# Arc tangent of the first unit ahead of its decay sums, one h chunk in a bank of attention, new due times

## The chip, the cores and the metric

The kernel runs on one core of one Trainium2 chip. The metric is the device time of one execution in microseconds (us). Five engines work side by side, each through its own list of instructions: TensorE (PE, matrix products), ScalarE (ACT, functions of one element from a table of functions that has to be loaded), VectorE (DVE), GpSimd (POOL, hardly used here) and SyncE (SP, which issues the transfers). An engine takes its instructions strictly in the order of its list; an instruction that waits holds back all behind it.

## The reference

There are two stages. The first is a gated linear attention over 4 batches, 8 heads, 768 steps and 48 dimensions: a complex state per head is turned and shrunk by a gate at every step, k times v is added to its real part, and q reads it.

```python
mag = np.sqrt(a_re * a_re + a_im * a_im)
scale = np.minimum(mag, 0.999) / (mag + 1e-06)
a_re_n, a_im_n = (a_re * scale, a_im * scale)
for t in range(S):
    new_re = ar * S_re - ai * S_im
    new_im = ar * S_im + ai * S_re
    S_re, S_im = (new_re + kv, new_im)      # kv = outer product of k_t and v_t
    y[:, :, t] = np.einsum('bhd,bhde->bhe', q[:, :, t], S_re)
```

Its result, 3072 tokens of 384, goes through two matrix products with a smooth ramp between: `h = x @ w_in` (384 to 2048), `g = h` where h >= 1, 0 where h <= -1 and `(h + 1)**2 / 4` between, and `out = g @ w_out`.

## The kernel before

**Units, blocks, gates.** The 3072 tokens are cut into 12 units of 256 steps of one batch; two units make a block of 512 tokens, and there are six blocks. `gates(u)` works out a unit's gate: the logarithm of its size (the decay) and its angle. Instead of stepping through time it forms running sums of both. For units 0 and 1 (`by_token`) PE does that with a triangular matrix of ones (`running`, L772, tile `tri`), for the others DVE does it with a scan (L798). From a sum of decays come exponentials (ACT, L826 for units 0 and 1), from a sum of angles sine and cosine, and DVE multiplies q and k by them (L840, L935). The gated heads `hd` are laid out anew by transfers on SP (L505).

**The function tables.** Ln and Exp live in one table set, arc tangent and sine in another. `table(name)` (L515) loads a set on ACT; L1418 loads the first. In `gates`, Ln, Exp, Square, Ln, Exp (all recorded by the helper `ac`, L715) work out the decay, with products on DVE between them (L729, L736, L745); the arc tangent needs the slope (imaginary over real part) that L729 makes. In this kernel `gates(0)` and `gates(1)` are generators that stop at `yield`; the last lines of the program step them in turn, with the table loads between, so that units 0 and 1 share each load.

**Attention.** `attend(u)` computes for each half of a unit the scores (L1089), masks them on DVE (L1101), transposes k (L1029), multiplies with v (L1141), reads the state (L1133) and updates it (L1058; the state is added up on DVE, L1068 and L1070). Its results lie in six banks of PSUM: `at0` to `at2` and `o0` to `o2`. `split` moves the values into the shape of tokens and cuts them into a rounded part xH (ACT, L1236) and a remainder xL (DVE, L1243).

**The two products.** `moe(blk)` works through 16 chunks f of 128 columns of h. `gemm1(f)` (L1269) is nine matrix products of 128x512 (three pieces, each xH by two parts of the weight and xL by one) into one of two banks, `h0` and `h1`, taken in turn; ACT makes s from h (L1295), DVE makes g from h and s (L1314, the last reader of the bank), ACT rounds it (gh, L1328), DVE takes the remainder (gl, L1332), and `gemm2` (L1346) adds gh and gl by w_out into `o0` to `o2`. In block 0 the first two chunks (HALVES = 2) are worked in halves, one per unit.

**Weights.** They arrive coded; `weights` decodes a piece in three steps on DVE (L535, L544, L553), rounds it on ACT (L559) and, for the first five pieces, forms the remainder on PE (L573 and L574, in bank `h0`), copied by ACT (L588); for later pieces DVE forms it (L564).

**What sets the order.** Nothing is issued as written. `Plan` records every operation with its cost, its engine and what it needs, works out backwards when each is due, and then lets each engine take, of what is ready, the operation due first. The table NUDGE adds a number of nanoseconds to the due time of the operation with that index. `emit` writes the order out and fills gaps of PE's plan with filler products (`warm`, L1409: a 128x128 product into bank `h1` that nobody reads) until the first chunk of h.

## Time and profile before

| what | us |
|---|---|
| median of three runs | 565.61 |
| the three runs | 565.61, 563.85, 566.46 |
| the profiled execution | 562.77 |
| its span, first to last instruction | 561.0 |
| PE busy in it | 549.5 |
| DVE busy | 438.1 |
| ACT busy | 396.1 |

The profile is of one execution. "Busy" counts the time in which an engine worked on something, filler products too. PE's matrix products are pipelined: one record starts before the one before it has ended, so durations of a row may add up to more than the time from one row's start to the next; the starts tell how long a group took. A 128x128 product of full precision leaves two records in the trace, so 41 filler products are 82 records. A bracket at the end of a row gives the idle time of the engine before it and the instruction that ended it.

### The profile page before, as it was taken

The page shows a single profiled execution, that of the slowest core. Times are in us where ns is not written, and L with a number is a line of the kernel's source. Part 1 is how long each engine was busy: PE and PEld are TensorE (multiplying, and loading weights), DVE is VectorE, ACT ScalarE, POOL GpSimd, SP SyncE. Part 2 cuts the span into 40 slices and gives each one's busy share as a digit, 9 for nine tenths or more (in the row PEclk, how much of TensorE's full clock was granted, in tenths as well). Part 3 has the DMA queues.
Part 4 walks back from the last instruction along what each step waited for, and adds up shares of the span by engine and source line. Part 5 has one row for each costly group of instructions (what it writes and reads, how often), then busy time and mean ns, then how long its engine had stood idle before and what let it go on. Part 6 is the DMA issues. An engine that isn't in the chain of part 4 may idle for free.

```text
span 561.0 us, 10737 instructions
## 1 busy us (share of the span) xinstructions
PE 549.5 (98%) x4256; PEld 461.1 (82%) x4256; DVE 438.1 (78%) x611; ACT 396.1 (71%) x638; POOL 4.1 (1%) x27
## 2 busy tenths in 40 slices
PE   8999799999999999999999999999999999999997
PEld 8978688788788888888888888888888888888885
DVE  5899999999978798788897758796888645445554
ACT  6987998989976667757757565557665752369973
POOL 2000000000000000000000000000000000000000
PEclk9999999999999999999999999999999999999999
DMA  8678384554711705405300552602635400087613
GB/s 339 251 231 270 115 288 163 177 220 161 227 58 49 224 4 154 158 21 147 129 1 4 160 169 76 200 2 66 209 115 161 171 1 1 27 317 276 232 63 110
DMA packets 23686, 80.56 MB, mean 144 GB/s; under 512 B 4560, under 2 KB 10320, under 8 KB 23632
## 3 DMA queue, kind: packets, MB, share of 16 engines
q1 hardware_dynamic: 23488, 79.71, 43.0%
q8 instruction: 34, 0.56, 0.4%
q14 instruction: 20, 0.16, 0.1%
q10 hardware_dynamic: 144, 0.13, 0.1%
HBM read 55.05 MB, written 4.72 MB: 107 GB/s over the span
## 4 chain that ended last, share of the span: by engine, by line
PE 84%; DVE 7%; DMA 4%; SPq 2%; ACT 1%; issue 1%; POOL 0%; DVEq 0%; POOLq 0%; ACTq 0%
PE o L1346 33%; PE h L1269 32%; PE at L1089 4%; PE idle L1409 3%; PE at L1133 3%; PE at L1141 3%; PE at L1058 2%; SPq L505 2%; DMA raw_o<-in_wl_dram 2%; PE at L1029 1%; PE o L772 1%; DMA out_dram<-ob 1%; DVE g L1314 1%; DMA kq<-in_kq_dram 1%; DVE x L935 1%
## 5 line engine op out<-in xcount | busy, mean ns | idle before, releaser
L1269 PE MATMUL h<-xH,wi 128*128 128x512 f32 (+1 forms) x588 | 181.3, 390 | 4.0 <-DVE g L1314 3.4
L1346 PE MATMUL o<-gh,wo 128*128 128x512 f32 x576 | 179.7, 393 | 0.0
L1269 PEld LDWEIGHTS h<-xH,wi 128*128 128x128 f32 x588 | 107.5, 188 | 27.3 <-DVE g L1314 4.2
L1346 PEld LDWEIGHTS o<-gh,wo 128*128 128x128 f32 x576 | 106.8, 188 | 22.5 <-DVE wo L564 0.5
L1269 PE MATMUL h<-xL,wi 128*128 128x512 f32 (+1 forms) x294 | 113.7, 387 | 0.0
L1346 PE MATMUL o<-gl,wo 128*128 128x512 f32 x288 | 112.3, 390 | 0.0
L1328 ACT CAST gh<-g 128x512 fp32r<-128x512 f32 x96 | 59.5, 620 | 56.5 <-DVE g L1322 27.4
L1314 DVE TENSOR_TENSOR g<-h,s 128x512 f32<-128x512 f32 x96 | 65.9, 686 | 40.2 <-ACT s L1295 38.3
L1295 ACT ACTIVATE s<-h,cst 128x512 f32<-128x512 f32 x96 | 65.6, 686 | 36.7 <-PE h L1269 28.2
L1332 DVE TENSOR_TENSOR gl<-g,gh 128x512 fp32r<-128x512 f32 x96 | 65.4, 684 | 26.9 <-PE o L1346 21.1
L1269 PEld LDWEIGHTS h<-xL,wi 128*128 128x128 f32 x294 | 55.2, 188 | 11.7 <-DVE xL L1243 0.4
L1346 PEld LDWEIGHTS o<-gl,wo 128*128 128x128 f32 x288 | 54.1, 188 | 11.3
L1322 DVE SCALAR_TENSOR_TENSOR g<-s,g 128x512 f32<-128x512 f32 x80 | 55.2, 690 | 2.1
L715 ACT ACTIVATE ai<-ai 128x768 f32<-128x768 f32 x48 | 40.2, 844 | 10.6 <-DVE ai L878 5.0
L1101 DVE COPY_PREDICATED am<-tri,at 128x512 f32<-128x512 uint32 x44 | 31.9, 740 | 7.7 <-PE at L1089 7.1
L798 DVE TENSOR_TENSOR_SCAN ai<-again,ai 128x768 f32<-128x768 uint8 x20 | 35.0, 1750 | 0.3
L1089 PEld LDWEIGHTS at<-hd 96*64 96x64 f32 x704 | 31.3, 137 | 3.9 <-issue 3.2
L1089 PE MATMUL at<-hd 96*64 96x128 f32 (+1 forms) x704 | 33.9, 249 | 0.0
L1141 PE MATMUL at<-am,V 128*64 128x128 f32 x352 | 32.9, 273 | 0.1
L1133 PE MATMUL at<-hd,st 96*64 96x128 f32 x304 | 30.5, 278 | 0.1
L515 ACT ACT_TABLE_LOAD x23 | 29.5, 1283 | 0.4
L715 ACT ACTIVATE x<-ai 128x768 f32<-128x768 f32 x27 | 22.1, 840 | 8.8 <-DVE ai L798 8.5
(127 smaller groups left out, 637.5 us busy)
## 6 DMA issues: line engine op xcount, KB each, us to landing
chk<-in_wl_dram SPq DMA_DIRECT2D x16, 768.0 KB, 5.4
kq<-in_kq_dram SPq DMA_DIRECT2D x12, 768.0 KB, 4.8
ai<-in_ari_dram SPq DMA_DIRECT2D x10, 768.0 KB, 6.0
V<-in_v_dram SPq DMA_DIRECT2D x12, 576.0 KB, 4.1
hd<-x SPq DMA_DIRECT2D x24, 288.0 KB, 3.3
hd<-kq SPq DMA_DIRECT2D x24, 288.0 KB, 4.2
raw_i<-in_wl_dram SPq DMA_DIRECT2D x8, 768.0 KB, 5.5
raw_o<-in_wl_dram SPq DMA_DIRECT2D x8, 768.0 KB, 6.0
```

Of the source, the lines that this page charges most:

```text
L715: lambda: A_.activation(out(), src(), f, **kw),
L798: lambda: V_.tensor_tensor_scan(dst().rearrange("p j t -> p (j t)"), again, src().rearrange("p j t -> p (j t)"), 0.0, op0=ALU.mult, op1=AL ...
L1089: PE_.matmul(SC.get()[o : o + HC, i + e, HC * k :], t[:, 0, ks], t[:, 1, qs], start=True, stop=True,)
L1133: PE_.matmul(o_, st.get().rearrange("p h e -> p (h e)")[:, lo : lo + 64], head(h)[:, 1, cs], start=True, stop=False,)
L1141: PE_.matmul(o_, V.get()[:, c, lo : lo + 64], ams[pr // 2].get()[:, 2 * (pr % 2) + e, :], start=st is None, stop=True,)
L1269: PE_.matmul(H.get()[:, lo:hi], weight["i", f // 2].get()[:, f % 2, part, sl], x.get()[:, j, lo:hi], start=j == 0 and n == 0, stop=j == NJ ...
L1295: lambda: A_.activation(SS.get(), H.get(), AF.Relu, bias=c_half, scale=-0.5 if spare else 0.5),
L1314: lambda: V_.tensor_tensor(G.get(), H.get(), SS.get(), op=ALU.max),
L1322: lambda: V_.scalar_tensor_tensor(G.get(), SS.get(), 1.0, G.get(), op0=ALU.min, op1=ALU.mult),
L1328: pl.op("ACT", act(T), lambda: A_.copy(GH.get(), G.get()), r=[G], w=[GH])
L1332: lambda: V_.tensor_tensor(GL.get(), G.get(), GH.get().bitcast(F32), op=ALU.subtract),
L1346: PE_.matmul(PO[m].get(), weight["o", f // 2].get()[:, f % 2, part, sl], g.get(), start=f == 0 and n == 0, stop=f == NF - 1 and n == 2,)
```

## The change

There are three edits. First, `gates(0)` stops twice more: its Square, and its arc tangent right behind, now come behind the slope's product (L729) with a load of the angle table ahead and a load of the logarithm table after them. So there are two more table loads, 24 become 26 with the first one. The remaining steps of `gates(0)` are recorded ahead of the last ones of `gates(1)`. Second, in block 0 chunk f=2 (SIDE) takes its bank from attention's three in turn (here `at0`) instead of from h's two; the chunks behind it take `h0` and `h1` in turn, so chunk 3 has `h0` and chunk 4 `h1`. Third, the table NUDGE has other numbers throughout, with which the planner puts all engines' work in another order.

```diff
@@ NUDGE
-    18: 15300, 20: -28200, 60: -152000, 61: 9200, 68: -300, 70: 500, 71: -17000, 96: -113000,
...
+    13: -203753000000, 17: -203724995000, 27: -896426000, 28: -202829000000, 29: -202829000000,
...
 HALVES = 2
+SIDE = (2,)
@@ gates
         ve(dve(N), lambda: V_.tensor_tensor(I(), I(), A(), op=ALU.mult), [a], [i])
+        if u == 0:
+            yield
         ac(A, I, AF.Square, [i], [a])
+        if u == 0:
+            ac(I, I, AF.Arctan, [a], [i], True)
+            yield
...
         if u > 1:
             table("trig_and_small")
+        if u > 1:
+            arctan()
         if u != 1:
-            arctan()
             yield
@@ gemm1
-            H = tl(turn_of("h", 2), [P, T], F32, f"h_{blk}_{f}", ps)
+            slot = turn_of(*("at", 3) if blk == 0 and f in SIDE else ("h", 2))
+            H = tl(slot, [P, T], F32, f"h_{blk}_{f}", ps)
@@ the end of the program
     first, second = gates(0), gates(1)
     next(first)
+    table("trig_and_small")
+    next(first)
+    table("natural_log_exp_and_others")
+    next(first)
     next(second)
     next(first)
     table("trig_and_small")
     next(first)
     next(second)
+    list(first)
     table("natural_log_exp_and_others")
     next(second)
     table("trig_and_small")
-    list(first)
     attend(0)
     list(second)
     attend(1)
```

In the rows of the two orders that follow, a tile's name has its number behind it, and the line numbers of the kernel after are smaller by 13 to 24, since its table is shorter.

PE at the start of the program, before. `idle` is the filler, `ai_0` and `ai_1` are the gates of units 0 and 1, `tri` the triangle of ones; `o0` and `o1` take the sums of decays, `o2` and `at2` those of angles:

```order
L1409 MATMUL idle_171<-tri_69,ident_64 128x128 x41
L772 MATMUL o0_112<-tri_69,ai_0_132 128x256
L772 MATMUL o0_112<-tri_69,ai_0_132 128x128
L772 MATMUL o0_112<-tri_69,ai_0_132 128x256
L772 MATMUL o0_112<-tri_69,ai_0_132 128x128
L772 MATMUL o1_113<-tri_69,ai_0_132 128x256
L772 MATMUL o1_113<-tri_69,ai_0_132 128x128
L1409 MATMUL idle_171<-tri_69,ident_64 128x128 x15
```

and after:

```order
L1392 MATMUL idle_167<-tri_69,ident_64 128x128 x41
L753 MATMUL o2_114<-tri_69,ai_0_132 128x256
L753 MATMUL o2_114<-tri_69,ai_0_132 128x128
L753 MATMUL o2_114<-tri_69,ai_0_132 128x256
L753 MATMUL o2_114<-tri_69,ai_0_132 128x128
L753 MATMUL at2_111<-tri_69,ai_0_132 128x256
L753 MATMUL at2_111<-tri_69,ai_0_132 128x128
L1392 MATMUL idle_167<-tri_69,ident_64 128x128 x18
L753 MATMUL o0_112<-tri_69,ai_0_132 128x256
```

The angle sums of unit 0 (o2, at2) have moved ahead of 18 fillers, and the decay sums (o0, o1), which stood right behind the first filler, come after them. The sums of unit 1, which were among the first, now come later, between products of weights' remainders.

ACT at the start, before (`x_0` and `x_1` are the decays of the two units, written by Ln):

```order
L715 ACTIVATE x_0_151<-ai_0_132,cst_86 128x3x256
L715 ACTIVATE ai_0_132<-x_0_151 128x768
L715 ACTIVATE ai_0_132<-ai_0_132 128x768
L715 ACTIVATE ai_0_132<-ai_0_132,cst_86 128x768
L715 ACTIVATE x_1_161<-ai_1_135,cst_86 128x3x256
L715 ACTIVATE ai_1_135<-x_1_161 128x768
L715 ACTIVATE x_0_151<-x_0_151,cst_86 128x3x256
L715 ACTIVATE ai_1_135<-ai_1_135 128x768
L715 ACTIVATE ai_1_135<-ai_1_135,cst_86 128x768
```

and after:

```order
L691 ACTIVATE x_0_151<-ai_0_132,cst_86 128x3x256
L691 ACTIVATE ai_0_132<-x_0_151 128x768
L491 ACT_TABLE_LOAD
L691 ACTIVATE ai_0_132<-ai_0_132 128x768 x2
L491 ACT_TABLE_LOAD
L691 ACTIVATE ai_0_132<-ai_0_132,cst_86 128x768
L691 ACTIVATE x_1_220<-ai_1_139,cst_86 128x3x256
L691 ACTIVATE ai_1_139<-x_1_220 128x768
L691 ACTIVATE x_0_151<-x_0_151,cst_86 128x3x256
```

Two table loads now stand around unit 0's Square and arc tangent (the row with x2). Unit 1's steps have moved behind them. Later in the list, between unit 0's exponentials and attention, ACT has three table loads, as before. Up to attention four weight pieces are cast instead of three, two of them ahead of unit 0's exponentials; the last copies of remainders before the first scores are those of weight i2, where before they were those of o0.

On SP, the first loads were those of the gates of units 0 and 1, then kq of unit 0, then weights i0 and i1; after, the gate of unit 0, weights i0 and i1, then the gate of unit 1, kq of unit 0 and weight i2.

PE at chunk 2 of block 0, before (the end of the second halves of chunks 0 and 1, then chunk 2 and the first products by w_out):

```order
L1269 MATMUL h_0_1_692<-xH_0_638,wi_0_289 128x256 x2
L1269 MATMUL h_0_1_692<-xL_0_682,wi_0_289 128x256
L1269 MATMUL h_0_2_778<-xH_0_638,wi_1_309 128x512 x2
L1269 MATMUL h_0_2_778<-xL_0_682,wi_1_309 128x512
L1269 MATMUL h_0_2_778<-xH_0_638,wi_1_309 128x512 x2
L1269 MATMUL h_0_2_778<-xL_0_682,wi_1_309 128x512
L1269 MATMUL h_0_2_778<-xH_0_638,wi_1_309 128x512 x2
L1269 MATMUL h_0_2_778<-xL_0_682,wi_1_309 128x512
L1346 MATMUL o0_112<-gh_0_0_784,wo_0_346 128x512 x2
```

and after:

```order
L1252 MATMUL h_0_1_737<-xH_0_683,wi_0_254 128x256 x2
L1252 MATMUL h_0_1_737<-xL_0_711,wi_0_254 128x256
L1252 MATMUL at0_109<-xH_0_683,wi_1_227 128x512 x2
L1252 MATMUL at0_109<-xL_0_711,wi_1_227 128x512
L1252 MATMUL at0_109<-xH_0_683,wi_1_227 128x512 x2
L1252 MATMUL at0_109<-xL_0_711,wi_1_227 128x512
L1252 MATMUL at0_109<-xH_0_683,wi_1_227 128x512 x2
L1252 MATMUL at0_109<-xL_0_711,wi_1_227 128x512
L1252 MATMUL h_0_3_813<-xH_0_683,wi_1_227 128x512 x2
L1252 MATMUL h_0_3_813<-xL_0_711,wi_1_227 128x512
L1252 MATMUL h_0_3_813<-xH_0_683,wi_1_227 128x512 x2
```

Chunk 2 has gone from a bank of h to `at0`, and chunk 3 in `h0` follows it at once, ahead of the products by w_out.

DVE from the end of attention of units 0 and 1 to g of chunk 0, before (L887 `state` stands just ahead of the first row):

```order
L1243 TENSOR_TENSOR xL_0_682<-xr_0_442,xH_0_638 128x3x256
L535 TENSOR_SCALAR y_i3_689<-raw_i3_482 128x768
L544 SCALAR_TENSOR_TENSOR raw_i3_482<-raw_i3_482,y_i3_689 128x768
L553 SCALAR_TENSOR_TENSOR raw_i3_482<-raw_i3_482 128x768
L1243 TENSOR_TENSOR xL_0_682<-xr_0_442,xH_0_638 128x256
L935 TENSOR_TENSOR x_2_380<-kq_2_475,ai_2_153 128x1536
L1243 TENSOR_TENSOR xL_0_682<-xr_0_442,xH_0_638 128x256 x2
L935 TENSOR_TENSOR kq_2_475<-kq_2_475,ai_2_153 128x1536
L564 TENSOR_TENSOR wi_3_755<-raw_i3_482,wi_3_755 128x2x384
L1070 TENSOR_TENSOR st_1_611<-st_1_611,o0_112 96x384
L1314 TENSOR_TENSOR g_0_0_771<-h_0_0_718,s_0_0_760 128x512
```

and after (`st` is the state's sum, `xL` the remainder of x, `kq` and `x` the turned q and k of unit 2, `raw` and `y` steps of decoding weights):

```order
L1052 TENSOR_TENSOR st_1_637<-st_1_637,o0_112 96x384
L869 TENSOR_SCALAR state_108<-ai_2_158 128x3
L1225 TENSOR_TENSOR xL_0_711<-xr_0_467,xH_0_683 128x3x256
L540 TENSOR_TENSOR wi_3_662<-raw_i3_375,wi_3_662 128x2x384
L520 SCALAR_TENSOR_TENSOR raw_o2_605<-raw_o2_605,y_o2_705 128x768
L917 TENSOR_TENSOR x_2_405<-kq_2_529,ai_2_158 128x1536
L1225 TENSOR_TENSOR xL_0_711<-xr_0_467,xH_0_683 128x256 x3
L917 TENSOR_TENSOR kq_2_529<-kq_2_529,ai_2_158 128x1536
L705 TENSOR_TENSOR ai_3_532<-ai_3_532 128x768
L529 SCALAR_TENSOR_TENSOR raw_o2_605<-raw_o2_605 128x768
L1297 TENSOR_TENSOR g_0_0_805<-h_0_0_722,s_0_0_777 128x512
```

The state's sum, which stood just ahead of g, now comes first; the decoding of weight i3 has been done earlier, and a product of unit 3 (L705) and steps of weight o2 stand ahead of g.

## Rows read from the trace of the kernel before

**Rows 1.** From the page: busy time of the engines (share of the span, instructions), and the granted clock of PE in 40 equal slices of the span, in tenths of full speed (9 is 90% or more).

```profile
PE 549.5 (98%) x4256; PEld 461.1 (82%) x4256; DVE 438.1 (78%) x611; ACT 396.1 (71%) x638; POOL 4.1 (1%) x27
...
PEclk9999999999999999999999999999999999999999
```

**Rows 2.** PE's timeline from the start to the first scores. Columns: start, time until the group's end, engine, line, operation, output from inputs, shape, count of records, idle time before.

```profile
1.82 11.74 PE L1409 MATMUL idle<-tri,ident 128*128 128x128 f32 x82 [1.82 <-POOL tri masks.py:66]
13.40 2.13 PE L772 MATMUL o<-tri,ai 128*128 128x256 f32 x12
15.36 3.51 PE L1409 MATMUL idle<-tri,ident 128*128 128x128 f32 x30
18.81 2.88 PE L772 MATMUL o<-tri,ai 128*128 128x256 f32 x16
...
37.04 1.56 PE L1089 MATMUL at<-hd 96*64 96x128 f32 x32
```

**Rows 3.** ACT's timeline up to attention, the same columns.

```profile
8.74 0.92 ACT L715 ACTIVATE x<-ai,cst 128x768 f32<-128x768 f32 x1
...
14.91 1.09 ACT L826 ACTIVATE x<-o 128x512 f32<-128x512 f32 x2 [1.53 <-PE o L772]
...
16.83 0.94 ACT L715 ACTIVATE x<-x,cst 128x768 f32<-128x768 f32 x1
17.78 1.28 ACT L515 ACT_TABLE_LOAD   x1
19.08 1.58 ACT L715 ACTIVATE ai<-ai 128x768 f32<-128x768 f32 x2
...
21.97 1.73 ACT L826 ACTIVATE x<-o 128x512 f32<-128x512 f32 x4
...
27.45 0.94 ACT L715 ACTIVATE ai<-ai,cst 128x768 f32<-128x768 f32 x1
...
35.46 0.48 ACT L588 CAST wo<-rest_o 128x384 fp32r<-128x384 f32 x1 [0.37 <-PE rest_o L574]
```

**Rows 4.** ACT's instructions grouped by line and shape over the whole span. Columns: group and count, busy us and mean ns of one, idle us before.

```profile
L715 ACT ACTIVATE ai<-ai 128x768 f32<-128x768 f32 x48 | 40.2, 844 | 10.6 <-DVE ai L878 5.0 <-DVE ai L729 3.3 <-DMA ai<-in_ari_dram 2.1
L515 ACT ACT_TABLE_LOAD x23 | 29.5, 1283 | 0.4
...
L559 ACT CAST wi<-raw_i 128x768 fp32r<-128x768 f32 x8 | 7.3, 906 | 0.1
...
L588 ACT CAST wi<-rest_i 128x384 fp32r<-128x384 f32 x6 | 2.8, 469 | 1.2 <-PE rest_i L574 1.2
```

**Rows 5.** PE's timeline from the end of attention of units 0 and 1 to the first product by w_out.

```profile
59.10 0.94 PE L573 MATMUL rest_o<-raw_o,ident 128*128 128x384 f32 x2
...
60.06 0.40 PE L1269 MATMUL h<-xH,wi 128*128 128x256 f32 x2
...
66.43 0.28 PE L1269 MATMUL h<-xL,wi 128*128 128x256 f32 x1
69.35 0.73 PE L1269 MATMUL h<-xH,wi 128*128 128x512 f32 x2 [2.64 <-DVE g L1314]
...
71.52 0.62 PE L1346 MATMUL o<-gh,wo 128*128 128x512 f32 x2
```

**Rows 6.** SP's issues of the moves of unit 0's heads and of the last moves of x before block 0.

```profile
31.24 3.43 SPq L505 DMA_DIRECT2D hd<-kq  x5
...
58.81 3.81 SPq L505 DMA_DIRECT2D xr<-xr  x6
```

**Rows 7.** PE's two later waits for DVE.

```profile
109.28 0.72 PE L1269 MATMUL h<-xH,wi 128*128 128x512 f32 x2 [0.54 <-DVE g L1314]
...
332.80 0.73 PE L1269 MATMUL h<-xH,wi 128*128 128x512 f32 x2 [0.21 <-DVE g L1314]
```

**Rows 8.** DVE's timeline: the first step on unit 0's angle sums, and the stretch from the end of attention to g of chunk 0 and a little behind.

```profile
22.36 0.68 DVE L854 TENSOR_SCALAR ai<-o 128x512 int32<-128x512 f32 x1
...
59.13 0.17 DVE L887 TENSOR_SCALAR state<-ai 128x3 f32<-128x3 f32 x1
59.44 0.96 DVE L1243 TENSOR_TENSOR xL<-xr,xH 128x768 fp32r<-128x768 f32 x1
...
63.11 1.75 DVE L935 TENSOR_TENSOR x<-kq,ai 128x1536 f32<-128x1536 f32 x1
64.77 0.75 DVE L1243 TENSOR_TENSOR xL<-xr,xH 128x256 fp32r<-128x256 f32 x2
...
67.11 0.95 DVE L564 TENSOR_TENSOR wi<-raw_i,wi 128x768 fp32r<-128x768 f32 x1
67.98 0.54 DVE L1070 TENSOR_TENSOR st<-st,o 96x384 f32<-96x384 f32 x1
68.60 0.69 DVE L1314 TENSOR_TENSOR g<-h,s 128x512 f32<-128x512 f32 x1
69.21 0.55 DVE L535 TENSOR_SCALAR y_o<-raw_o 128x768 uint32<-128x768 uint32 x1
69.67 0.95 DVE L729 TENSOR_TENSOR ai<-ai 128x768 f32<-128x768 f32 x1
```

**Rows 9.** Two stretches: its bounds, its length, busy us (and instructions) of PE, PE's weight loads, DVE, ACT and POOL, granted clock, share of the transfer engines, GB/s.

```profile
4.13:35.94 31.81, 30.60 (x204) 27.34 (x203) 25.33 (x35) 26.88 (x37) 0.77 (x4) 1.00 0.76 288
5.00:10.00 5.00, 5.00 (x39) 5.00 (x39) 1.92 (x2) 3.82 (x6) 0.00 (x0) 1.00 1.01 412
```

87 rows, old and new, of the table NUDGE are left out of this document.

## The prediction

> **What bounds the kernel now.** I read the page's busy shares first [rows 1]: TensorE (PE) is busy for 98% of the span at a granted clock that reads 9 (90% or more) in all 40 slices, so an edit pays only if it takes work or a wait from PE. The waits of PE come next: 2.64 us before chunk 2 of block 0 [rows 5], 0.54 and 0.21 us later [rows 7], all ended by DVE's product g. The rest of PE's loss is idle filler (L1409) in the opening and counts as busy, so it is seen only in PE's row of time: 82 filler records until 13.40 and 30 more from 15.36 [rows 2]. Behind the gap of 2.64 us PE has work in hand until the end but for those two small waits. The time is therefore set by when the gap's end is reached and by what PE has done by then; I work out that one point for both kernels.
>
> **The opening: decay sums later.** Before, unit 0's decay sums stand directly behind the first filler, at 13.40, and 30 filler records follow them. After, the angle sums stand there (possible because the arc tangent comes early), then 18 fillers (36 records), and only then the decay sums. Twelve records of sums cost 15.36 - 13.40 = 1.96; a filler record costs 3.45/30 = 0.115 (15.36 to 18.81). So the decay sums start at 13.40 + 1.96 + 36 x 0.115 = 19.5, which is 6.1 later. ScalarE's (ACT's) first exponential of a decay comes 14.91 - 13.40 = 1.51 behind the sums' start, so at 21.0, and they end as before 16.83 - 14.91 = 1.92 later, at 22.9 [rows 2, 3].
>
> **The two table loads.** One is 1.283 us, with the next activation right behind it (17.78 + 1.28, then 19.08) [rows 3, 4]. I cost the pair, 2.57, at nothing, because ACT waits there for PE's sums: everything that ACT has to do before the exponentials is ready earlier. The last piece hangs on DVE: angle sums end at 15.36, DVE's step on them takes 0.68, then a product of 0.95 [rows 8], then Square 0.84, Ln 0.94 and a cast 0.91 [rows 3, 4], which gives 19.7 against 21.0. Unit 1's inputs are now queued on SP behind two weight loads of 768 KB; at the 412 GB/s of that stretch [rows 9] these are 1.9 us each, and what needs them first (8.7 before) slips to 12.5 at the most, still ahead. If that cover of 1.3 us is gone, the loads cost up to 1.3 us of the 2.57.
> The Trainium skill, "ScalarE: Activation LUTs", section "What ACT_TABLE_LOAD costs", gives about 1283 ns for the load and about 1380 ns of drain at every switch of set. The rows above show the first figure and no drain. By the Trainium skill the two early loads would be 2.76 us more of ACT, so 22.4 against 21.0, and the end 1.4 later.
>
> **ACT up to attention.** Behind unit 0's exponentials ACT now has, until the copy of the first half of weight i2's remainder: two Ln or sine steps with a pointer (0.94), seven copies of remainders (0.47), three table loads (1.283), five activations of 0.844, two casts (0.906) and unit 1's exponentials (1.73) [rows 3, 4]: 1.88 + 3.29 + 3.85 + 4.22 + 1.81 + 1.73 = 16.8. It ends at 22.9 + 16.8 = 39.7. Before, the matching copy (wo) ended at 35.46 + 0.48 = 35.94, with ACT busy for 26.9 of the 31.8 us up to there [rows 3, 9]. From that copy to the first scores were 37.04 - 35.94 = 1.10; after, four fillers more (8 x 0.115 = 0.9): attention starts at 41.7, that is s = 4.7 later. The other bound on that start is the moves of unit 0's gated heads: their cosine ends at 22.9 + 8.0 = 30.9 against 28.4, so they land 2.5 later than before, at 39.6 if the last was as late as 37.04 [rows 3, 6]; it does not decide. So s lies between 0 (PE's later sums fully absorbed, the floor if everything else is as before) and 6.1 (all passed on); the sum of ACT's durations gives 4.7 and I take it.
>
> **From attention to the gap.** Attention of units 0 and 1 took 59.10 - 37.04 = 22.06 with two remainder products in it; it has two afterwards as well, so it ends at 63.8, and h0 begins after 1.15 of filler instead of 0.96 of remainder products [rows 5]. What PE then waits for is bank h0, freed by DVE's g0. Behind attention's end DVE has: state sum 0.54, state 0.17, xL 0.96, a weight sum 0.95, a decode step 0.95, the turn of x 1.75, three xL of about 0.4, the turn of kq 1.75, a product 0.95, a decode step 0.95, g0 0.69 [rows 8]: 10.8 of durations; rows of DVE overlap by about 0.08 (63.11 + 1.75 against 64.77), ten times 0.8, so 10.0. The last moves of x (SP, 58.81 + 3.81 before [rows 6]) come 4.7 later too and can add some tenths at xL. I take 10.5: h0 is free at 74.3. Before, g0 ended at 68.60 + 0.69 = 69.29, 10.2 behind attention.
>
> **Chunk 2 in attention's bank.** Before, chunk 2 waited from 66.7 to 69.35 for h0 and was done at 71.52, that is 2.17. After, it needs no h bank: it runs inside the wait and chunk 3 is the one that waits, until 74.35. At 74.35 after stands where before stood at 71.52: the change is 74.35 - 71.52 = 2.8, or s - 1.9. The edit saves the 2.17 it can; the later opening costs more. Lower bound of this saving 0 (if DVE later makes PE wait for the same amount, the rival below), upper bound 2.17 plus the two later waits.
>
> **Behind the gap.** The new table reorders everything, and the two later waits cost before 0.54 and 0.21, some 0.9 with the slower products behind them (0.72 against the 0.62 of two such products undisturbed) [rows 5, 7]. DVE's next two g's are due close together: g1 comes 4.8 behind g0 (two products of 0.95 and a third, 0.55, two of 0.69), PE has 2.2 + 2.1 for it; a wait of 0.5 is likely. Gains of 0.9 and losses of 2 are both possible; I take a loss of 0.3.
>
> **Sum.** 4.7 - 1.9 + 0.3 = 3.1 to 3.2. Against the profiled execution: 562.77 + 3.2 = 566.0. The median of the runs is 565.61, 2.84 above that execution, so the forecast is 568.8 us. Own range of this case 567 to 571.
>
> **Rivals.**
> 1. Attention starts only 2.5 later, set by the moves of the heads and not by ACT's list. For it: the scores at 37.04 show no wait for ACT's copy longer than the products between them [rows 2]. Against it: the last remainder product stands right before the scores on PE in both orders. Then 2.5 - 1.9 + 0.1 = 0.7: 566.4, no change.
> 2. Faster: the opening isn't later, s = 0, because ACT's list of 39.7 contains work that before had to be done after attention had started, and PE's sums are not what ACT waits for. The saving of 1.9 stays and the two later waits (0.9) go: -2.8 to -2.9, 562.7. It decides from s below 1.9; beyond the half per cent only at s near 0. For it: the gap of 2.64 is PE's largest wait [rows 5]. Against it: 6.1 us on PE's row [rows 2].
> 3. The saving is given back: DVE is what paces PE from the gap on, so a chunk done early only moves the wait to chunks 3 and 4. Then 2.2 comes back and the later waits grow by some tenths: +5.7, 571.3. For it: all three waits of PE end on DVE's g [rows 5, 7]. Against it: DVE is busy for 78% of the span [rows 1].
> 4. A drain at each load, as weighed above: 570.2.
>
> **How the numbers follow.** Half a per cent is 2.8 us, about what a measurement of this kernel can tell from no change. Chances: forecast 0.38 (just beyond 2.8 slower, so 0.24 of it slower and 0.14 the same), rival 1 0.26 (same), rival 2 0.20 (faster), rival 3 0.14 and rival 4 0.02 (slower). So faster 0.20, same 0.40, slower 0.40. The range 562.0 to 572.5 reaches rival 2's number and a microsecond beyond rival 3's, as the unknown waits ask; the likeliest's own is above.
>
> **What the profile of after would show.** Right: the angle sums on PE at about 13.4, decay sums near 19.5, table loads of 1.28 near 6 and 9 us on ACT, ACT's exponentials near 21, first scores near 41.7, chunk 2 in bank at behind the second halves with no wait, then a wait for g at about 74.3. Wrong: scores before 40 (rival 1 or 2), a wait of PE ended by DVE's g of over 2 us behind 75 (rival 3), idle time behind a table load (rival 4). If the decay sums start before 17, the filler was mispriced and everything moves earlier with it.

## The result and the profile after

The changed kernel takes **567.0 us** (median of 20 runs, 566.37 to 568.8); the kernel before, run beside it 20 times, takes 564.08 us (562.43 to 566.62). The ratio is 1.0052, 95% interval 1.0039 to 1.0065: slower by half a per cent. The forecast was 568.8 us in a range of 562.0 to 572.5. The profiled execution of after took 567.03 us with a span of 565.2 us, against 562.77 and 561.0 before: +4.2, where the forecast's sum said 3.1 to 3.2.

From the page of after: busy times and the granted clock of PE, and the group of table loads (to be read beside [rows 1] and [rows 4]).

```profile
PE 552.7 (98%) x4280; PEld 462.5 (82%) x4280; DVE 440.5 (78%) x611; ACT 396.3 (70%) x640; POOL 4.1 (1%) x27
...
PEclk9999999999999999999999999999999999999999
...
L491 ACT ACT_TABLE_LOAD x25 | 32.1, 1283 | 0.4
```

PE's busy time has grown by 3.2 us (24 records of filler more, that is 12 products), DVE's by 2.4 with the same 611 instructions, ACT has its two loads. PE is as full as before, so the 4.2 us are read from its timeline. PE's timeline of after (start, time, engine, line, operation, shape, count, idle time before), the rows that answer to [rows 2] and [rows 5], and the last product:

```profile
1.82 10.81 PE L1392 MATMUL idle<-tri,ident 128*128 128x128 f32 x82 [1.82 <-POOL tri masks.py:66]
12.47 1.47 PE L753 MATMUL o<-tri,ai 128*128 128x256 f32 x8
...
14.43 4.18 PE L1392 MATMUL idle<-tri,ident 128*128 128x128 f32 x36
18.45 2.13 PE L753 MATMUL o<-tri,ai 128*128 128x256 f32 x12
...
40.09 1.56 PE L1071 MATMUL at<-hd 96*64 96x128 f32 x32
...
62.17 1.38 PE L1392 MATMUL idle<-tri,ident 128*128 128x128 f32 x10
...
64.34 0.39 PE L1252 MATMUL h<-xL,wi 128*128 128x256 f32 x1 [0.55 <-DVE xL L1225]
...
68.08 0.38 PE L1252 MATMUL h<-xL,wi 128*128 128x256 f32 x1 [1.34 <-DVE xL L1225]
...
70.09 0.63 PE L1252 MATMUL at<-xH,wi 128*128 128x512 f32 x2
...
72.76 0.73 PE L1252 MATMUL h<-xH,wi 128*128 128x512 f32 x2 [0.43 <-DVE g L1297]
...
559.59 0.39 PE L1329 MATMUL o<-gl,wo 128*128 128x512 f32 x1
```

The order is the one forecast: angle sums first, 36 filler records, decay sums, scores, chunk 2 in bank at with no wait in front of it, then chunk 3 waiting for g. One thing has to be taken out before rows are compared: what follows the same 82 filler records starts at 12.47 here and at 13.40 before [rows 2], 0.93 sooner. In the eleven traces in which they were unchanged it started anywhere from 12.47 to 13.92, since the first of them run at twice the later spacing for a time that differs from run to run (in these two traces until 4.54 and until 6.46 us). So I count from the end of that filler. By it the scores start 27.62 us behind (40.09 - 12.47) against 23.64 before (37.04 - 13.40), **4.0 later**; chunk 3 starts where before the first product by w_out stood [rows 5] 60.29 behind against 58.12, **2.2 later**; and the last product by w_out, at 559.59 against 556.31, is **4.2 later**. In raw times these are 3.05, 1.24 and 3.28; the rest of the span's 4.2 is at the very end, where the last output transfer landed 2.8 us behind its issue, 1.7 before. That end belongs to the order and not to chance: in the seven traces whose program ends as after's does, the span runs on for 5.6 to 5.9 us from the start of the last product by w_out, in the six that end as before's does for 4.7. It is 1.0 us for which the forecast has no term.

The 2.64 us in front of chunk 2 [rows 5] are gone as one wait and stand there as three, 0.55, 1.34 and 0.43: 2.3 us. PE now waits for DVE's xL before it comes to g.

ACT's timeline of after up to the scores, beside [rows 3]:

```profile
5.94 1.28 ACT L491 ACT_TABLE_LOAD   x1
7.24 1.72 ACT L691 ACTIVATE ai<-ai 128x768 f32<-128x768 f32 x2
8.98 1.28 ACT L491 ACT_TABLE_LOAD   x1
...
19.96 0.60 ACT L807 ACTIVATE x<-o 128x512 f32<-128x512 f32 x1 [1.31 <-PE o L753]
...
21.88 0.38 ACT L807 ACTIVATE x<-o 128x256 f32<-128x256 f32 x1 [0.23 <-DVE state L796]
22.16 0.93 ACT L691 ACTIVATE x<-x,cst 128x768 f32<-128x768 f32 x1
22.98 0.47 ACT L564 CAST wi<-rest_i 128x384 fp32r<-128x384 f32 x1
...
37.64 0.46 ACT L564 CAST wi<-rest_i 128x384 fp32r<-128x384 f32 x1
```

Both loads stand where the forecast put them, with 0.02 us behind the first (5.94 + 1.28 against 7.24), and ACT still waits 1.31 us for the decay sums: the loads are hidden. Look also at the ends: 22.16 + 0.93 is 23.09, and the next row starts at 22.98. Rows of ACT overlap by about 0.1 us.

DVE around the first g, beside [rows 8], and the stretch from 4.2 us to the end of g as one row of windows for each kernel (bounds, length, busy us of PE, PEld, DVE, ACT and POOL with counts, granted clock, DMA share, GB/s).

```profile
65.07 0.95 DVE L520 SCALAR_TENSOR_TENSOR raw_o<-raw_o,y_o 128x768 uint32<-128x768 uint32 x1
...
71.15 0.95 DVE L529 SCALAR_TENSOR_TENSOR raw_o<-raw_o 128x768 uint32<-128x768 uint32 x1
72.02 0.68 DVE L1297 TENSOR_TENSOR g<-h,s 128x512 f32<-128x512 f32 x1
```

After:

```profile
4.20:72.70 68.50, 64.02 (x680) 56.15 (x679) 61.04 (x81) 59.36 (x85) 0.69 (x4) 1.00 0.72 250
```

Before:

```profile
4.20:69.29 65.09, 60.42 (x647) 52.86 (x646) 57.90 (x77) 55.12 (x82) 0.70 (x4) 1.00 0.70 246
```

By the end of g of chunk 0, DVE has done 61.04 us of work in after and 57.90 before. It idled 7.46 and 7.19 us. The g ends 3.41 later in raw time, with four instructions more ahead of it (81 against 77, 3.14 us), decode steps of a tile of w_out among them (65.07, 71.15), and hardly more waiting.

### The profile page after: what moved, and what is told of

It is laid out like the page before. It is cut to its first block, busy times and chain, and to the rows that moved or that the text cites. A ratio compares the mean times of both kernels' runs of the same rounds, so it can differ in the third digit from the quotient of the medians.

```text
span 565.2 us, 10742 instructions
## 1 busy us (share of the span) xinstructions
PE 552.7 (98%) x4280; PEld 462.5 (82%) x4280; DVE 440.5 (78%) x611; ACT 396.3 (70%) x640; POOL 4.1 (1%) x27
## 4 chain that ended last, share of the span: by engine, by line
PE 78%; DVE 11%; DMA 4%; ACT 3%; SPq 1%; issue 1%; POOL 0%; DVEq 0%; POOLq 0%; ACTq 0%
PE h L1252 31%; PE o L1329 31%; PE at L1071 4%; PE idle L1392 3%; PE at L1115 3%; PE at L1123 3%; PE at L1040 2%; DMA raw_i<-in_wl_dram 1%; SPq L481 1%; PE at L1011 1%; DVE g L1297 1%; DMA out_dram<-ob 1%; DVE kq L821 1%; DVE x L917 1%; DVE am L1083 1%
## 5 line engine op out<-in xcount | busy, mean ns | idle before, releaser
L1252 PEld LDWEIGHTS h<-xH,wi 128*128 128x128 f32 x582 | 106.1, 188 | 24.1 <-DVE g L1297 3.5
L1252 PE MATMUL h<-xL,wi 128*128 128x512 f32 (+1 forms) x291 | 112.5, 387 | 1.9 <-DVE xL L1225 1.9
```

Source lines behind the costliest of these rows:

```text
L1252: PE_.matmul(H.get()[:, lo:hi], weight["i", f // 2].get()[:, f % 2, part, sl], x.get()[:, j, lo:hi], start=j == 0 and n == 0, stop=j == NJ ...
```

## The experiments

Each kernel below has the order of the named kernel written out as a list, with a table of filler counts, in place of the due times, so that an edit moves nothing but itself. The rewriting alone was not timed; four_early_loads, whose list is that of after with two loads put in, gives after's ratio to the digit. All were timed in five rounds beside the kernel before, three or four kernels to a chip; before's medians on the three chips were 564.04, 564.02 and 564.01 us, so the ratios stand beside one another. A ratio is the measurement's own estimate and not the quotient of the two medians; the two differ by up to 0.2%. The diffs show the edit alone, without the lists.

**bank_h_again.** After's order, with the third chunk back in a bank of h. For it chunks 2, 3 and 4 each move one place back in PE's list: chunk 2 behind the wait, chunk 3 behind three products by w_out, chunk 4 behind the next scores.

```diff
-SIDE = (2,)
+SIDE = ()
```

> The kernel after in its own order of instructions, but chunk 2 of block 0 is put back into a bank of h, so that chunk 2 waits for g of chunk 0, chunk 3 for g of chunk 1, and what can't stand where it did moves back as little as possible. Theory (the bank saves the time of one chunk inside the wait): chunk 2 starts where chunk 3 started in after (72.8), PE is 2.0 to 2.2 later from there on and to the end: about 569.1, 0.4% over after. Rival (DVE paces block 0, a chunk done early only moves the wait): within 0.5 us of after's 567.0.

Measured: 570.7 us (570.5 to 571.01), ratio 1.0123 (1.0101 to 1.0145): 3.7 above after. PE's timeline:

```profile
74.21 0.73 PE L1347 MATMUL h<-xH,wi 128*128 128x512 f32 x2 [2.50 <-DVE g L1392]
...
83.79 0.73 PE L1347 MATMUL h<-xH,wi 128*128 128x512 f32 x2 [1.36 <-DVE g L1392]
```

The wait of before is back at chunk 2, and a second stands in front of chunk 4. The first filler ends at 13.92 in this trace, 1.45 later than in after's; counted from there, the last product (563.24) comes 2.2 later, which is the saving that the forecast gave the bank. The profiled run is itself the median of the four, and its late start and these 2.2 make up its 3.7; whether the other three started as late is open. By these runs the change without its bank is 1.2% slower than before.

**fewer_fillers_after.** 6 instead of 18 fillers in front of the decay sums.

```diff
-    35: 41, 23: 18, 202: 5,
+    35: 41, 23: 6, 202: 5,
```

> The kernel after in its own order, with 6 fillers instead of 18 between unit 0's angle sums and its decay sums. The decays are there at 16.8 (end of the DVE step L726), so the sums start at 16.9 and not at 18.45, and ACT, ready at 18.65, starts the exponentials 1.3 earlier. Theory (the opening is a chain from PE's filler over the exponentials to attention and to the end): first scores 1.3 earlier, at about 38.8, and the time 1.3 shorter, 565.7. Rival (DVE's list sets when g of chunk 0 comes): scores earlier, g of chunk 0 and the end where they were, 567.0 within 0.3.

Measured: 566.05 us (565.22 to 566.9), ratio 1.0033 (1.0018 to 1.0048): 0.95 below after. PE's timeline:

```profile
17.38 2.23 PE L848 MATMUL o<-tri,ai 128*128 128x256 f32 x12 [0.96 <-DVE ai L821]
...
39.14 1.56 PE L1166 MATMUL at<-hd 96*64 96x128 f32 x32
```

The decay sums now wait 0.96 for their input instead of standing behind fillers, the exponentials on ACT follow with no wait, and the scores stand 26.18 behind the first sums instead of 27.62: 1.44 earlier. DVE's g of chunk 0 comes 1.27 earlier by the same count (71.24 - 12.96 against 72.02 - 12.47), and by the medians two thirds of the 1.44 reach the end. So far as this edit shortens it, the opening passes through, as the forecast's term s said.

**opening_of_before.** The order of before up to the second halves, that of after behind, with chunk 2 in bank at: the change without its later opening.

```diff
+SIDE = (2,)
...
-            H = tl(turn_of("h", 2), [P, T], F32, f"h_{blk}_{f}", ps)
+            slot = turn_of(*("at", 3) if blk == 0 and f in SIDE else ("h", 2))
+            H = tl(slot, [P, T], F32, f"h_{blk}_{f}", ps)
```

> The instructions up to the second halves of chunks 0 and 1 in the order of the kernel before (no early arc tangent, no two more table loads), and everything behind them in the order of after, chunk 2 in a bank of attention. Theory (the late start of attention is what the change costs): first scores at about 37, and the time 3 us shorter than after, 564. Rival (what costs is the DVE work that the new order puts ahead of g of chunk 0, 61.0 us of it against 57.9 in before): scores at 37, g of chunk 0 all the same near 72, time as after, 567 within 0.5.

Measured: 569.06 us (567.54 to 569.97), ratio 1.0088 (1.0067 to 1.0109), slower than after. PE's timeline:

```profile
70.69 0.58 PE L1341 MATMUL h<-xL,wi 128*128 128x256 f32 x1 [4.59 <-DVE xL L1314]
...
73.20 0.63 PE L1341 MATMUL at<-xL,wi 128*128 128x512 f32 x1
73.63 1.05 PE L1341 MATMUL at<-xH,wi 128*128 128x512 f32 x2
```

The scores start at 37.30, as before, and all of it is lost in one wait of 4.59 for DVE's xL. Then something I had not reckoned with: behind the wait the products come at 0.43 us each and not at 0.23 (73.20 to 73.63). Windows of the same kernel, in the columns above:

```profile
64.00:68.00 4.00, 2.10 (x16) 1.70 (x14) 1.88 (x3) 3.74 (x5) 0.00 (x0) 1.00 0.56 197
68.00:72.00 4.00, 1.31 (x6) 1.31 (x7) 4.00 (x6) 0.69 (x1) 0.00 (x0) 0.59 0.35 69
72.00:76.00 4.00, 4.00 (x13) 3.23 (x13) 3.44 (x6) 3.94 (x6) 0.00 (x0) 0.56 1.03 290
76.00:80.00 4.00, 4.00 (x19) 3.30 (x18) 4.00 (x6) 3.33 (x7) 0.00 (x0) 1.00 0.95 229
```

The granted clock is 1.00 until 68, 0.59 and 0.56 from 68 to 76, and 1.00 again behind: it fell to its lower level, 1.2 GHz, during the wait and stayed there for some microseconds of work.

**dve_steps_behind_g.** The four steps that stand ahead of g on DVE in after, moved behind it. DVE's order, after and edited:

```diff
-TENSOR_SCALAR y_o<-raw_o 128x768
 TENSOR_TENSOR xL<-xr,xH 128x3x256
 TENSOR_TENSOR wi<-raw_i,wi 128x2x384
-SCALAR_TENSOR_TENSOR raw_o<-raw_o,y_o 128x768
 TENSOR_TENSOR x<-kq,ai 128x1536
 TENSOR_TENSOR xL<-xr,xH 128x256 x3
 TENSOR_TENSOR kq<-kq,ai 128x1536
+TENSOR_TENSOR g_0<-h_0,s_0 128x512
 TENSOR_TENSOR ai<-ai 128x768
+TENSOR_SCALAR y_o<-raw_o 128x768
+SCALAR_TENSOR_TENSOR raw_o<-raw_o,y_o 128x768
 SCALAR_TENSOR_TENSOR raw_o<-raw_o 128x768
-TENSOR_TENSOR g_0<-h_0,s_0 128x512
```

> The kernel after in its own order, with four DVE steps (three of decoding weight o2, 0.55 and two of 0.95, and the product L705 of unit 3, 0.95) put directly behind g of chunk 0 instead of ahead of it. Theory (only the wait before chunk 3 counts): that wait of 0.4 goes, g of chunk 0 comes about 0.7 earlier, as ACT ends s of chunk 0 at 71.4, and the time falls by 0.4, to 566.6. Rival (DVE paces PE for the whole of block 0's first chunks): the 3.1 us come back as waits of PE behind chunk 3 and the time grows by 2 to 3 us, 569 to 570.

Measured: 570.62 us (569.51 to 570.8), ratio 1.0115 (1.0095 to 1.0135): 3.6 above after. DVE's timeline of it:

```profile
72.28 0.69 DVE L1392 TENSOR_TENSOR g<-h,s 128x512 f32<-128x512 f32 x1 [1.59 <-ACT s L1387]
...
77.68 0.68 DVE L1410 TENSOR_TENSOR gl<-g,gh 128x512 fp32r<-128x512 f32 x1
```

And PE's:

```profile
78.42 0.62 PE L1424 MATMUL o<-gl,wo 128*128 128x512 f32 x1 [2.40 <-DVE gl L1410]
78.84 1.05 PE L1424 MATMUL o<-gh,wo 128*128 128x512 f32 x2
```

With 3.4 us of steps less ahead of it, g comes only 0.8 earlier (72.28 - 13.52 against 72.02 - 12.47): DVE then waits 1.59 for ACT's s, which in after was ready at 71.36, 0.66 ahead of g. DVE's list and ACT's list reach this g almost together, so neither alone is its price. The steps do not go away either: gl now stands behind them, PE waits 2.40 for it, and the clock falls (78.42 to 78.84, 0.42 for one product). Counted from the filler's end, PE is 2.0 us behind after when this wait ends (78.42 - 13.52 against 75.38 - 12.47), and at 80.97 it is 3.2 behind (76.74 in after): the wait is the larger part, the clock the smaller. The rival, DVE pacing PE here, held.

**bank_at_in_before.** The reverse: before's order, with chunk 2 in bank at and the products by w_out of chunk 0 behind chunk 3. PE's order, before and edited:

```diff
-MATMUL h_2<-xH,wi 128x512 x2
-MATMUL h_2<-xL,wi 128x512
...
-MATMUL o<-gh_0,wo 128x512 x2
-MATMUL o<-gl_0,wo 128x512
...
+MATMUL at<-xH,wi 128x512 x2
+MATMUL at<-xL,wi 128x512
...
 MATMUL h_3<-xH,wi 128x512 x2
...
+MATMUL o<-gh_0,wo 128x512 x2
+MATMUL o<-gl_0,wo 128x512
```

> The kernel before in its own order, with one edit: chunk 2 of block 0 in a bank of attention, chunk 3 right behind it and ahead of the products by w_out, and g of chunk 2 a little earlier on DVE. Theory of the prediction (the bank saves one chunk's time, 2.17, inside the wait of 2.64): PE reaches the end 2 us earlier, 562, 0.35% under before. Rival (given back: the bank is held until g of chunk 2 and unit 2's transposes wait for it, DVE paces): the wait goes at chunk 2 and a new one of 2 to 2.5 us stands before the transposes of unit 2; time 564 to 565.5, same as before or 0.2% over.

Measured: 566.54 us (565.85 to 567.69), ratio 1.0035 (1.0015 to 1.0055): the bank alone makes before slower, by more than the rival's range. PE's timeline:

```profile
69.37 0.73 PE L1341 MATMUL h<-xH,wi 128*128 128x512 f32 x2 [0.81 <-DVE g L1386]
...
78.35 1.54 PE L1100 MATMUL at<-ident,hd 96*128 96x96 f32 x8 [2.84 <-DVE g L1386]
79.60 1.20 PE L1418 MATMUL o<-gh,wo 128*128 128x512 f32 x2
```

Chunk 2 runs at 66.33 with no wait, and the wait of 2.64 shrinks to 0.81. Nine microseconds on, the transposes of the next unit want the borrowed bank, which chunk 2's own g has not yet freed: 2.84 us. Counted from the filler's end, these transposes start 1.3 later than in before (78.35 - 13.21 against 77.21 - 13.40). More is lost behind them: the granted clock is 0.50 from 80 to 84 us, two products take 1.20 where they took 0.71 in before (at 77.88), and the product that stands at 84.63 (80.60 in before) is by the same count 4.2 later. All twelve runs had a mean clock of 0.996 or less. So the saving is given back, as rival 3 has it, but by another mechanism: the bank is due back too soon, and the clock falls at that wait. What the bank would cost here at a full clock was not tried.

**four_early_loads.** After with two more table loads beside the two added ones.

```diff
-    table("trig_and_small")
+    pl.op("ACT", TABLE, lambda: [nc.scalar.preload_act_table_set(name) for name in
+        ("trig_and_small", "natural_log_exp_and_others", "trig_and_small")], w=[TAB])
```

> The kernel after in its own order with two table loads more in front of unit 0's Square and arc tangent (three there instead of one, and one behind), 2.57 us more of ACT. Theory (hidden: ACT waits 1.3 us for the decay sums, and before that for unit 1's gate and for DVE): exponentials of unit 0 no later than 0.3 behind the decay sums' place in after, time as after, 567.0 within 0.5. Rival (the pair costs what is not covered, and the pair of the change did so too): 1.2 to 2.6 us more, 568.2 to 569.6.

Measured: 567.37 us (565.64 to 568.15), ratio 1.0052 (1.0033 to 1.0071): after's ratio. ACT's timeline:

```profile
5.91 3.86 ACT L1504 ACT_TABLE_LOAD   x3
9.78 1.72 ACT L786 ACTIVATE ai<-ai 128x768 f32<-128x768 f32 x2
...
21.05 0.60 ACT L902 ACTIVATE x<-o 128x512 f32<-128x512 f32 x1 [1.35 <-PE o L848]
```

2.57 us more on ACT and still 1.35 of waiting for the sums. ACT's earlier waits for inputs took 1.5 of them up: it is ready at 19.70 instead of 18.65. The filler ended 1.09 later here than in after's trace (13.56), so by the same count 0.26 of the wait would be left: the loads are hidden, the doubled ones just so. Three loads in a row take 3 x 1.286, with 0.01 behind the last.

**fewer_fillers_before.** Before, with 33 fillers at the start instead of 41.

```diff
-    20: 41, 34: 15,
+    20: 33, 34: 15,
```

> The kernel before in its own order, with 33 fillers instead of 41 ahead of unit 0's decay sums. The decays are there at 12.4 (11.45 + 0.95 on DVE), the fillers ended at 12.5 to 13.9 in the traces so far. Theory (the opening is a chain to the end): sums 0.5 to 1 earlier, first scores by as much, time 563.3, 0.1 to 0.2% under before and under after. Rival (DVE's list absorbs it): 564.1 within 0.3.

Measured: 564.17 us (562.42 to 565.18), ratio 0.9984 (0.9968 to 1.0001). PE's timeline:

```profile
69.08 0.73 PE L1339 MATMUL h<-xH,wi 128*128 128x512 f32 x2 [3.08 <-DVE g L1384]
...
70.63 1.06 PE L1339 MATMUL h<-xH,wi 128*128 128x512 f32 x2
```

The scores start 0.7 earlier (36.33), the wait grows to 3.08, and the clock falls behind it (1.06 for the two products where 0.62 is undisturbed). In 11 of the 12 runs the mean granted clock was 0.997 or less. What the opening gives, the clock takes.

**late_order_of_before.** After's order through the first five chunks of block 0, then before's.

PE's order where the two part, after and edited:

```diff
-MATMUL o<-gh_2,wo 128x512 x2
-MATMUL o<-gl_2,wo 128x512
-MATMUL h_5<-xH,wi 128x512 x2
...
 MATMUL at<-ident,hd_0 128x96
...
 MATMUL at<-V,kT 64x48 x8
+MATMUL h_5<-xH,wi 128x512 x2
...
+MATMUL o<-gh_2,wo 128x512 x2
+MATMUL o<-gl_2,wo 128x512
```

> The kernel after in its own order through the opening, attention of units 0 and 1 and block 0's first five chunks, and everything behind in the order of the kernel before. Theory (the new table's order behind block 0's start costs the 2.0 us by which PE's lag grew between 73 us and the end): time 2 shorter than after, 565. Rival (that lag is DVE's work and attention's pieces, which must be done in either order): 567 within 0.7.

Measured: 567.04 us (566.36 to 567.79), ratio 1.004 (1.0023 to 1.0056), not to be told from after. What after loses behind the gap isn't the new table's later order. The trace tells where it is lost. PE's timeline:

```profile
113.02 0.73 PE L1347 MATMUL h<-xH,wi 128*128 128x512 f32 x2 [0.29 <-DVE g L1392]
```

In before this product stands at 109.28 [rows 7], and from there on the two kernels have one order. Counted from the filler's end (13.27 here) the lag is 2.2 at chunk 3, 3.9 here and 4.2 at the last product by w_out (560.42): 1.7 of the 2.0 us arise ahead of this product.

**gap_filled_in_before.** Before, with ten idle products (twenty records) into bank at in front of chunk 2, where PE waits 2.64.

```diff
+    def more():
+        G = banks["at0"][:, :P]
+        for _ in range(10):
+            PE_.matmul(G, ident, mask, start=True, stop=True)
```

> The kernel before in its own order, with ten filler products (2.3 us) in attention's bank at0 inside PE's wait of 2.64 ahead of chunk 2; chunk 2 itself starts when it did. Theory (the runs of before that took 565.6 to 567.0 are those in which PE's granted clock fell after that wait; their mean clock is 0.993 or 0.994, against 0.998 and more in those of 562.1 to 564.3): no run below 0.996 any more, and the median at that of the runs with full clock, 563.0, 0.2% under before. Rival (the two groups have another cause): times as before, median 564.0, both groups present.

Measured: 563.89 us (562.88 to 564.76), ratio 0.9993 (0.9973 to 1.0012). The median did not move to the theory's 563.0. What went is the upper end: of the 23 runs of before on this chip, five were above 565.7 with a mean granted clock of 0.994 or less, and nine more had 0.995 to 0.997; of the twelve filled runs all had 0.998 or more. Why the fillers' median lies 0.75 above that of before's nine runs at that clock (563.14) stays open; in its trace 0.7 us of lag arise far behind, from 333 to 336 us, where PE waits 0.38 and 0.28 for DVE's g and in before 0.21 once [rows 7].

**gap_filled_fewer_fillers.** The two together: 33 fillers at the start and twelve idle products in the wait.

```diff
-    20: 41, 34: 15,
+    20: 33, 34: 15,
...
-        for _ in range(10):
+        for _ in range(12):
```

> The same with twelve filler products in the wait (which was 3.1 us here), and with 33 fillers instead of 41 ahead of unit 0's decay sums. Theory (opening 0.7 earlier, clock kept): no run below 0.996, median 562.3, 0.3% under before and 0.8% under after. Rival: as the kernel with 33 fillers alone, 564.1.

Measured: 562.58 us (562.09 to 563.44), ratio 0.9973 (0.9957 to 0.999): faster than before by 0.3%, and by 0.8% than after. PE's timeline:

```profile
66.19 2.84 PE L1488 MATMUL at<-tri,ident 128*128 128x128 f32 x24
69.52 0.74 PE L1341 MATMUL h<-xH,wi 128*128 128x512 f32 x2 [0.49 <-DVE g L1386]
...
70.32 0.63 PE L1341 MATMUL h<-xH,wi 128*128 128x512 f32 x2
```

The wait of 3 us is filled but for 0.49, and behind it two products take 0.63 again and not 1.06. All twelve runs had a granted clock of 0.998 or more. By the medians the shorter opening pays once the clock is kept: 1.3 less than its twin with 41 fillers (gap_filled_in_before). The traces don't show where, since chunk 2 starts at 69.52 here and at 69.46 there. Against before's own nine runs at that clock (563.14) the gain is 0.6, which so few runs don't tell from nothing; the larger part of the 0.3% is the clock's.

**opening_of_before_filled.** opening_of_before with eighteen idle products in its wait of 4.6, to part that kernel's two losses.

```diff
+    def more():
+        G = banks["at0"][:, :P]
+        for _ in range(18):
+            PE_.matmul(G, ident, mask, start=True, stop=True)
```

> The kernel with the opening of before and the order of after behind it, with 18 filler products (4.1 us) in bank at0 inside PE's wait of 4.6 for xL. Theory (of its 2.0 us over after, the fallen clock is all; what is left is DVE's work, the same as in after): 567.0 within 0.5, mean clock 0.997 or more. Rival (the order itself is 2 us worse than after's): 569 as before.

Measured: 568.6 us (567.44 to 569.98), ratio 1.0086 (1.0058 to 1.0114), with clocks of 0.998 and more in all six runs. The clock was not what made that kernel slow. DVE's timeline:

```profile
67.00 0.56 DVE L608 TENSOR_SCALAR y_o<-raw_o 128x768 uint32<-128x768 uint32 x1 [2.25 <-DMA raw_o<-in_wl_dram]
...
73.42 0.68 DVE L1388 TENSOR_TENSOR g<-h,s 128x512 f32<-128x512 f32 x1
```

Scores at 36.60, and g at 73.42, 60.4 behind the first sums (12.98), against 59.6 in after with scores 4 us later. DVE's work from 4.2 us to the end of g is that of after (60.92 us, 61.04 there), and a decode step in it waits 2.25 for its load. That wait is this kernel's own. SP's issue of that load here, and in after:

```profile
62.44 0.51 SPq L593 DMA_DIRECT2D raw_o<-in_wl_dram  x1
```

```profile
54.84 1.18 SPq L496 DMA_DIRECT2D raw_o<-in_wl_dram  x1
```

Up to here SP has the order of before, and DVE works ahead in that of after. Without the wait g could come up to 2.25 sooner, 58.2 behind the first sums, where fewer_fillers_after has it at 58.3. So with DVE's work as in after, an attention that starts 4 us earlier is worth at most some 1.4 us at this g (an estimate from these rows); a kernel with the early opening and the early load was not built.

## Why the prediction was right, and where not

**The sign and the likeliest case held**: slower by half a per cent, with an opening that is later by more than the bank saves. That the size fits as well (2.9 by the medians, 3.2 forecast) is luck in part: the opening was put 0.7 too late, the part behind the gap 1.7 too short, the end of the program (1.0) was left out, and three in five of before's runs lose time to the clock, which the forecast did not know. How much of the 2.9 the later opening itself costs is not shown: 1.44 of it taken away bring 0.95 (fewer_fillers_after), and no run takes it away whole without a new wait. Taken from the end of the first filler, the chain came out step by step:

| step | forecast | measured |
|---|---|---|
| decay sums, behind the first filler's end | 6.1 | 5.98 (18.45 - 12.47) |
| sums to first exponential | 1.51 | 1.51 (19.96 - 18.45) |
| first exponential to ACT's next row | 1.92 | 2.20 (19.96 to 22.16) |
| ACT's list up to the last copy | 16.8 | 15.94 (22.16 to 38.10) |
| copy to scores | 2.0 | 1.99 (38.10 to 40.09) |
| **s** | **4.7** | **4.0** |
| attention | 22.06 | 22.08 (40.09 to 62.17) |
| attention's end to h0 free | 10.5 | 10.53 (62.17 to 72.70) |
| exit of the gap | +2.8 | +2.2 |
| behind the gap, to the last product by w_out | +0.3 | +2.0 |
| from there to the end of the span | not in the sum | +1.0 |

**ACT's list was mis-sized.** Step "ACT up to attention" added bare durations, 16.8; it took 15.94. I let DVE's rows overlap by 0.08 in the next step and forgot it for ACT, where the rows above do so by 0.1. Against that the exponentials took 0.28 longer, with two waits of 0.23 for DVE where before had one of 0.29. -0.86, +0.28 and -0.12 at the sums are the whole of 4.7 against 4.0.

**The loads are hidden, with no drain**: the same loads doubled changed nothing (four_early_loads). By the Trainium skill, "ScalarE: Activation LUTs", section "What ACT_TABLE_LOAD costs", a drain of about 1380 ns goes with each switch; no trace here agrees, 0.02 us stand behind a load, and rival 4 falls.

**The bank saves 2.2 in after's order** (bank_h_again: 2.2 in the trace, 3.7 in the median), as "Chunk 2 in attention's bank" said. But the forecast gave the bank a price that it doesn't have by itself: in before's order the same edit loses 0.35%, since the borrowed bank is wanted back 9 us later and the clock falls at that wait (bank_at_in_before). That belongs to the table's order, and the forecast only allowed for it as rival 3.

**"From attention to the gap" gave the right number for half of the reason.** 10.5 behind attention held to 0.03 us. The step reads as though attention's start set g; opening_of_before and its filled twin start attention 4 us earlier, and g starts 60.3 and 60.4 behind the first sums, no sooner than after's 59.6. DVE's longer list sets it there, and 2.12 and 2.25 us of it are a wait for a load that stands in before's place on SP and is wanted in after's place on DVE; without that wait the list would allow about 58.2. dve_steps_behind_g shows a third bound, ACT's s, 0.66 us below. Three lists reach this g within some 1.4 us in after, and my chain happened to run along one of them.

**"Behind the gap" was wrong: +2.0 for +0.3.** The rows show part of it. PE's timeline of after, where DVE's gl and g are late by less than a wait that is listed:

```profile
80.91 0.73 PE L1329 MATMUL o<-gh,wo 128*128 128x512 f32 x2
81.74 0.50 PE L1329 MATMUL o<-gl,wo 128*128 128x512 f32 x1
```

Between the first and the second row lie 0.83 us where two such products undisturbed take 0.45: 0.38 lost, while DVE's gl runs until 81.68. In late_order_of_before 1.7 of the 2.0 lie between chunk 3 and 113 us, and it is not the later order. That DVE paces PE in this stretch is what dve_steps_behind_g shows: work put behind g comes back as a wait. Which of DVE's instructions would have to go was not tried, nor was PE's own order in this stretch, so the cause of the 2.0 is open beyond that. Rival 3's sum puts 2.9 there (5.7 less 2.8): two thirds of its price came, but not by its mechanism, for the bank's saving stays (bank_h_again).

**The absolute number was 1.8 too high, 1.5 of it by its base.** The forecast added 2.84, the distance of the profiled execution from a median of three. In 20 runs before's median is 564.08, 1.3 above that execution. The profiled execution was the better base. It is no chance value: over the 35 runs of before on one chip, 14 with a mean granted clock of 0.998 or more have a median of 562.97, 10 with 0.995 to 0.997 one of 564.12, and 11 with 0.994 or less one of 566.22. Of the first three runs two (565.61 and 566.46) lie in the range of the last kind. After's 14 runs at 0.998 or more have a median of 566.94. At a full clock, then, the change costs 4.0 us by the medians. The two profiled executions differ by 4.3; counted from the filler's end their traces differ by 5.2 (4.2 to the last product by w_out and 1.0 behind it), and why the runs show 1.2 less is open, with one trace of each. Three in five of before's runs show the lower clock, which brings the medians to 2.9 apart.

**Rivals 1 and 2** fall with s: 4.0, neither 2.5 nor 0. Rival 2 had the saving of the bank with no later opening; opening_of_before and bank_at_in_before are nearest to it, and both are slower than before.

## What to carry to other kernels

When a step moves, add up what each engine has to do ahead of the instruction that releases the wait, for DVE and ACT as well as for the engine that waits: where several lists arrive within a microsecond or so, shortening one brings only what the next one leaves (here 0.8 us for 3.4). A borrowed buffer must be free again when its owner wants it; that wait stands later and can be larger than the one saved (here 2.84 for 1.83). And price a wait of TensorE of some microseconds with the products behind it, which may run at half speed: here filling such a wait with idle products, and only then shortening the opening, gave the one version faster than both kernels, though it isn't told from the runs of before that kept their clock.

## What the runs showed of the hardware

I had not expected the granted clock to matter within a kernel whose page reads 9 in all slices. Behind PE waits of 4.59, 3.08, 2.84 and 2.40 us the trace shows products of 512 columns at about 0.43 us instead of 0.23 and a granted clock near half, until some microseconds of work had gone by (from 70.69 to 75.7 behind the wait of 4.59, from 78.35 to 84.9 behind that of 2.84); behind before's profiled wait of 2.64, bank_h_again's of 2.50, and after's 0.55, 1.34 and 0.43, the products kept 0.23. In before most runs show a lower mean clock than the profiled one, which fits the same wait being followed by the fall in some runs and not in others; a trace of such a run of before was not taken. A mean of 0.997 alone says little: in eleven of the thirteen traces the clock is also low in the last 0.4 to 2.9 us of the span, behind the last products (in before 0.67 from 559 to 561 us), and fewer_fillers_after's profiled run has 0.997 without any fall ahead of that. That the wait is the cause was shown by filling it: all 24 runs of the two kernels with before's order and fillers in the wait kept 0.998 or more, where 14 of before's 23 beside them did not. The Trainium skill, "TensorE: Matmul & The Clock Gate", section "HAM oscillation — how this bites in real kernels", describes the same: a wait lets the clock drop to half, and the next products begin at it. The traces agree behind three of the four waits; behind that of 3.08 the products came at 0.23 us for another 1.3 us (69.08 to 70.34) before they slowed.

The start has a spread of its own: the first fillers run at the wider spacing until 4.5 to 7.5 us, and whatever stands behind them starts up to 1.4 us sooner or later from run to run, which two single traces cannot tell from an effect of an edit unless they are counted from the fillers' end.
